# V and U on three shared pairs of PSUM banks, turned modes in the transpose banks, and no filler passes: a sparse-attention and spectral-mixing kernel

## The chip, the cores and the metric

The kernel runs on one core of one Trainium2 chip. The metric is device time in microseconds, the median of several runs. One further execution was recorded by the hardware profiler; it is the source of every time below that is not a median.

The names of the engines in the profile: PE is TensorE (matrix multiplication), PEld its weight loads, DVE is VectorE, ACT is ScalarE, POOL is GpSimd (here it mainly issues the loads that convert float32 to float16), SP issues the stores. PSUM is the small memory that TensorE writes its results to. It has eight banks here, each of 512 float32 values per partition; a "pair" below is two banks that one instruction of ScalarE or VectorE can read in one go.

## The reference

Two stages. First an attention over 8 batches, 8 heads, 576 tokens and 64 dimensions; the first four heads see the last 32 tokens, the last four every 32nd token. Then a spectral mixing of the attention's output `x` (8 x 576 x 512): a Fourier transform along the tokens, of which 64 modes are kept and each multiplied by its own complex 512 x 512 matrix, the inverse transform, and a last layer.

```python
def _attn_ref(q, k, v):
    # B, H, S, D = 8, 8, 576, 64; stride 32
    scores = scale * np.matmul(q, k.transpose(0, 1, 3, 2))
    mask_local = (rel >= 0) & (rel < stride)
    mask_strided = (rel >= 0) & (pos[None, :] % stride == pos[:, None] % stride)
    # ... heads 0 to 3 local, 4 to 7 strided; softmax
    return np.matmul(attn, v)

def _moe_ref(x, w_r, w_i, w_ch):
    X = np.fft.rfft(x, axis=1)
    Xr, Xi = (np.real(X[:, :n_modes]), np.imag(X[:, :n_modes]))   # n_modes = 64
    Yr = np.einsum('bmd,mde->bme', Xr, w_r) - np.einsum('bmd,mde->bme', Xi, w_i)
    Yi = np.einsum('bmd,mde->bme', Xr, w_i) + np.einsum('bmd,mde->bme', Xi, w_r)
    Y[:, :n_modes] = Yr + 1j * Yi
    y = np.fft.irfft(Y, n=S, axis=1)
    u = x + y
    return u + np.maximum(u @ w_ch, 0.0)
```

The weights of the modes, 2 x 64 x 512 x 512 float32 values, are most of what the kernel reads: 162.83 MB come from memory in all.

## The kernel before

In order of time the kernel does this:

1. The strided attention of the eight batches, while the first weights are loaded.
2. The local attention, interleaved with the first modes (`slot` 0), while weights stream in. Each batch ends with a DFT of its output.
3. More modes (`slot` 1), while `premix` prepares for each token tile its share of `x @ w_ch` (called v) and of `x` (xo), with the modes still missing.
4. The last stretch: the last 24 modes. Between them, `renew` adds the modes that are already there to v and xo. The last of the spectra is added in a final loop, which puts out `u + relu(v)` tile by tile. V stands for the accumulation of `u @ w_ch`, U for that of `u`.

PSUM is divided by pools, which change from stage to stage. The last stretch has one V pair, two U pairs and two y banks (2 + 4 + 2); when the modes are done, a second V pair, `v2`, takes the place of y.

```python
    def psum_pools(**bufs):
        pctx.close()
        for n, c in bufs.items():
            pss[n] = pctx.enter_context(
                tc.tile_pool(name="ps_" + n, bufs=c, space=PSUM)
            )
# ...
    psum_pools(y=2, tp=2, sc=2, av=2)      # stages 2 and 3
# ...
    psum_pools(v=1, u=2)                   # stage 4
    yctx = ctx.enter_context(ExitStack())
    pss["y"] = yctx.enter_context(tc.tile_pool(name="ps_y2", bufs=2, space=PSUM))
```

The DFT of a batch, and a pair of modes. Four modes (two pairs) accumulate in one y bank; ScalarE copies it out (`yr`), and `four_turned` turns the result with four small passes through another bank. `flush` calls it at the next odd mode.

```python
    def dft(b, half):
        # ...
        xp = psum("sc" if half else "y")
        # ... ten passes into xp, then four copies by ScalarE from xp to X

    def four_turned(slot, m0, yr):
        tr = psum("y")
        for e in range(4):
            nc.tensor.matmul(
                tr[:, ds(64 * e, 64)].rearrange("p (i x) -> p i x", i=4),
                yr[:, ds(128 * e, 128)],
                idn.rearrange("p (i x h) -> p h i x", i=4, h=2)[:, m0 // 32],
                start=True,
                stop=True,
            )
        # ...

    def mode_pair(slot, m):
        half = 1 - slot
        if m % 4 == 0:
            ypt[slot] = psum("y")
        yp = ypt[slot]
        # ... eight passes wt x X into yp (line 587)
        if slot or m // 2 not in GUEST:
            w_fetch()          # next weights, into the buffer now free
        if m % 4:
            yr = big.tile([128, DM], F16, tag="yr", name="yr")
            act_copy(yr, yp)
            queued.append(lambda: four_turned(slot, m - 2, yr))
```

The last 16 modes take another form: sixteen short passes each (line 620), with the weights as the stationary operand.

The last stretch: the late spectra, the filler and the renewal of one tile pair.

```python
    def spec_late(mm, kept, eng):
        up = psum("u", pair=True)
        for bq in range(2):
            mm(2, bq, up[:, bq])
        for b in range(B):
            eng(kept[b][64:96], up[ds(32 * (b % 4), 32), b // 4])

    def fill(acc, n):
        for _ in range(n):
            nc.tensor.matmul(acc, idn, v0s[0][:, 0], start=True, stop=True)

    def renew(b, ts):
        n = len(ts)
        if n == 2:
            v0, xo = v0s[b][:, ts[0] : ts[0] + 2], xos[b][:, ts[0] : ts[0] + 2]
        else:
            v0, xo = v0h[b // 2].unsqueeze(1), xoh[b // 2].unsqueeze(1)
        vp, up = psum("v", pair=True), psum("u", pair=True)
        if n == 1:
            fill(vp[:, 0], 3)
        for j, t in enumerate(ts):
            nc.tensor.matmul(vp[:, j], idn, v0[:, j], start=True, stop=False)
            rows_of(b, t, vp[:, j], zzs, False)
        act_copy(v0, vp[:, 0:n])
        for j, t in enumerate(ts):
            rows_of(b, t, up[:, j], yys, True)
        nc.vector.tensor_tensor(out=xo, in0=up[:, 0:n], in1=xo, op=AluOp.add)

    def spec_last():
        spec_late(spec_y, yys, lambda o, i: nc.vector.tensor_copy(out=o, in_=i))
        fill(psum("v", pair=True)[:, 0], 5)
```

In `renew`, the identity pass of V has line 949 in the profile, the passes of `rows_of` line 750, `fill` line 937, and the add line 954; `act_copy` has line 243 for all its callers.

The units of the final loop. Their identity passes have lines 985 (V) and 995 (U), those of `new_rows` line 1008. V and U of unit 0, and U of unit 1, are started before the last modes.

```python
    def v_early(k, stop=False):
        vps[k] = psum(("v", "v2")[k % 2], pair=True)
        v_own(k, stop)

    def u_early(k, times=1):
        ups[k] = psum("u", pair=True)
        rows = list(enumerate(own(items[k], xos, xoh)))
        for n, (j, r) in enumerate(rows * times):
            nc.tensor.matmul(
                ups[k][:, j], idn, r, start=True, stop=n < len(rows) * (times - 1)
            )
# ...
    rest = [(0, m) for m in range(SPLIT1, NM)] + [(1, m) for m in range(SPLIT0, NM)]
    n = 0
    NL = len(rest) - 2
    for i, (slot, m) in enumerate(rest):
        mode(slot, m)
        upto = min(len(late), i + 1)
        for w in late[n:upto]:
            w()
        n = upto
        if i == NL - 1:
            v_early(0)
            u_early(0)
        elif i == NL:
            u_early(1, times=3)
    yctx.close()
    # ... the last spectra (spec_z, spec_y), then:
    pss["v2"] = pctx.enter_context(tc.tile_pool(name="ps_v2", bufs=1, space=PSUM))
# ...
    for k in range(2, LAST + 2):
        if k <= LAST:
            v_early(k)
        # ... at k = 4 and 5 half of the V pair serves for the last spectrum
        if k > 2:
            u_early(k - 1)
        if k <= LAST:
            new_rows(k, vps[k], zzs)
        if k > 2:
            new_rows(k - 1, ups[k - 1], yys)
        if k <= LAST:
            v_done(k)          # ScalarE: relu(V)
        # ...
        if k > 2:
            u_done(k - 1)      # VectorE: U + relu(V), then the store
```

Of the kernel before, what the change touches and what calls it, by code (L numbers as in the profile page):

```python
# [56 lines left out]
def kernel(  # L57
# [10 lines left out]
    nc = tc.nc  # L68
# [6 lines left out]
    pss = {}  # L75
    pctx = ctx.enter_context(ExitStack())

    def psum_pools(**bufs):
        pctx.close()
        for n, c in bufs.items():  # L80
            pss[n] = pctx.enter_context(
                tc.tile_pool(name="ps_" + n, bufs=c, space=PSUM)
            )

    def psum(kind, half=False, pair=False):
        if pair:
            return pss[kind].tile([128, 2, 512], FP, tag=kind, name=kind)
        if half:
            return pss[kind].tile([128, 1024], F16, tag=kind, name=kind)
        return pss[kind].tile([128, 512], FP, tag=kind, name=kind)  # L90
# [19 lines left out]
    idn = cs["cI"]  # L110
# [11 lines left out]
    def spectra_tile(n):  # L122
        if n == "X0":
            Xh[0] = big.tile([128, 4, B, 2, NM], F16, tag=n, name=n)
        else:
            YS[n] = big.tile([128, 4, 4, 16, 16], F16, tag=n, name=n)
# [115 lines left out]
    def act_copy(out, in_):  # L242
        nc.scalar.activation(out=out, in_=in_, func=ACTF.Copy)  # L243
# [307 lines left out]
    def spectrum(slot, part, src):  # L551
        if slot == 0:
            nc.scalar.activation(out=YS["Y0"][part], in_=src, func=ACTF.Copy)
        else:
            nc.vector.tensor_tensor(
                out=YS["YT"][part], in0=src, in1=YS["Y0"][part], op=AluOp.add
            )

    def four_turned(slot, m0, yr):
        tr = psum("y")  # L560
        for e in range(4):
            nc.tensor.matmul(
                tr[:, ds(64 * e, 64)].rearrange("p (i x) -> p i x", i=4),
# [5 lines that stand above are left out]
        if slot == 0 and m0 == 0:  # L569
            spectra_tile("Y0")  # L570
        spectrum(
            slot,
            (slice(None), slice(None), m0 // 16, slice(None), ds(m0 % 16, 4)),
            tr[:, 0:256].rearrange("p (e i x) -> p e x i", e=4, i=4),
        )
# [28 lines left out]
    def mode(slot, m):  # L604
        half = 1 - slot
        if m % 2:
            flush()
        if slot == 0 or m < SPLIT0:
            if m % 2:
                mode_pair(slot, m - 1)  # L610
            return
        mi, mg = m % 8, m // 8
        if mi == 0:
            ypt[slot] = psum("y")
        yp = ypt[slot]
        yv = yp.rearrange("p (m e x) -> p m e x", m=8, e=4)
        wt = w_tiles[ORDER.index((half, m))]
        for e in range(4):
            for c in range(4):
                nc.tensor.matmul(  # L620
                    yv[:, mi, e, :],
                    wt[:, XC[c], ds(128 * e, 128)],
                    Xh[half][:, c, :, :, m],
                    start=(c == 0),
                    stop=(c == 3),
                )
        if m % 2:
            w_fetch()
        ends = {5: 6, 7: 2} if mg == 7 else {7: 8}
        if mi in ends:  # L630
            n = ends[mi]
            m0 = mi + 1 - n
            spectrum(
                slot,
                (slice(None), slice(None), mg // 2, slice(None), ds(8 * (mg % 2) + m0, n)),
                yp.rearrange("p (m e x) -> p e x m", m=8, e=4)[:, :, :, ds(m0, n)],
            )
# [54 lines left out]
    v0s, xos = {}, {}  # L692
# [51 lines left out]
    def rows_of(b, t, acc, spectra, fresh):  # L744
        if t < 4:
            todo = [(acc, out_cols(t), b)]
        else:
            todo = [(acc[ds(64 * j, 64)], ds(512, 64), b - 1 + j) for j in range(2)]
        for o, cols, bb in todo:
            nc.tensor.matmul(  # L750
                o, cA[0:96, cols], spectra[bb][0:96], start=fresh, stop=True
            )


    psum_pools(tp=3, sc=3, av=2)
    load_str(0, 1)
    const_load(nc.scalar, "cI", "cM6", "cM5")
# [66 lines left out]


    psum_pools(y=2, tp=2, sc=2, av=2)
    NMODES = [10, 8, 7, 7, 6, 6, 6, 6]
    for b in range(B):
# [12 lines left out]
        n = 0  # L841
        nm = NMODES[b]
        for mi in range(nm):
# [3 lines left out]
            n = upto  # L847
# [7 lines left out]
    xoh = [ptr.tile([128, DM], F16, name=f"xoh{i}") for i in range(4)]  # L855
# [58 lines left out]
    n = 0  # L914
    for m in range(SPLIT0):
# [4 lines left out]
        n = upto  # L920
        if m >= 16 and m % 16 in (2, 4):
            spec(m // 16 - 1, m % 16 // 2 - 1)

    psum_pools(v=1, u=2)
    yctx = ctx.enter_context(ExitStack())
    pss["y"] = yctx.enter_context(tc.tile_pool(name="ps_y2", bufs=2, space=PSUM))

    def spec_late(mm, kept, eng):
        up = psum("u", pair=True)
        for bq in range(2):  # L930
            mm(2, bq, up[:, bq])
        for b in range(B):
            eng(kept[b][64:96], up[ds(32 * (b % 4), 32), b // 4])

    def fill(acc, n):
        for _ in range(n):
            nc.tensor.matmul(acc, idn, v0s[0][:, 0], start=True, stop=True)

    def renew(b, ts):
        n = len(ts)  # L940
        if n == 2:
            v0, xo = v0s[b][:, ts[0] : ts[0] + 2], xos[b][:, ts[0] : ts[0] + 2]
        else:
            v0, xo = v0h[b // 2].unsqueeze(1), xoh[b // 2].unsqueeze(1)
        vp, up = psum("v", pair=True), psum("u", pair=True)
        if n == 1:
            fill(vp[:, 0], 3)
        for j, t in enumerate(ts):
            nc.tensor.matmul(vp[:, j], idn, v0[:, j], start=True, stop=False)
            rows_of(b, t, vp[:, j], zzs, False)  # L950
# [4 lines that stand above are left out]

    def spec_last():
        spec_late(spec_y, yys, lambda o, i: nc.vector.tensor_copy(out=o, in_=i))
        fill(psum("v", pair=True)[:, 0], 5)

    late = [lambda: spec_late(spec_z, zzs, act_copy), spec_last]  # L960
    for b in range(B):
        for t in (0, 2):
            late.append(lambda b=b, t=t: renew(b, (t, t + 1)))
        if b % 2:
            late.append(lambda b=b: renew(b, (4,)))

    def units_of(item):
        P, t = item
        return [(2 * P + j, t) for j in range(2 if t < 4 else 1)]

    items = []
# [5 lines left out]
    vps, ups, rls, osbs = {}, {}, {}, {}  # L977

    def own(item, kept, half):
        P, t = item  # L980
        return [kept[b][:, t] for b, _ in units_of(item)] if t < 4 else [half[P]]

    def v_own(k, stop=False):
        for j, r in enumerate(own(items[k], v0s, v0h)):
            nc.tensor.matmul(vps[k][:, j], idn, r, start=True, stop=stop)  # L985

    def v_early(k, stop=False):
        vps[k] = psum(("v", "v2")[k % 2], pair=True)
        v_own(k, stop)

    def u_early(k, times=1):
        ups[k] = psum("u", pair=True)
        rows = list(enumerate(own(items[k], xos, xoh)))
        for n, (j, r) in enumerate(rows * times):
            nc.tensor.matmul(  # L995
                ups[k][:, j], idn, r, start=True, stop=n < len(rows) * (times - 1)
            )

    def new_rows(k, acc, spectra):
        P, t = items[k]  # L1000
# [46 lines left out]
# [9 lines that stand above are left out]
            v_early(0)  # L1056
            u_early(0)
        elif i == NL:
            u_early(1, times=3)
    yctx.close()  # L1060
    with tc.tile_pool(name="ps_s", bufs=1, space=PSUM) as pss["s"]:
        zp = pss["s"].tile([128, 512], FP, name="zp")
# [16 lines left out]
# [3 lines that stand above are left out]
        if k == 4:  # L1082
            held = vps[k][:, 1]
            spec_z(3, 1, held)
        if k == 5:
            held = vps[k][:, 1]
            spec_y(3, 1, held)
# [7 lines that stand above are left out]
            v_done(k)  # L1095
        if k in (4, 5):
            act_copy((zzs, yys)[k - 4][1], held)
        if k > 2:
            u_done(k - 1)
# [31 lines left out]
```

The softmax here doesn't subtract the row's maximum and nothing guards it: scores larger than these inputs give would overflow.

## Time and profile before

| | |
|---|---|
| median of 3 runs | 432.15 us (431.37 to 432.51) |
| span of the profiled execution | 432.4 us |
| instructions | 9809 |
| mean granted TensorE clock | 0.935 |
| PE busy | 351.0 us (81%), 4188 passes |
| DVE busy | 235.3 us (54%) |
| ACT busy | 218.9 us (51%) |
| POOL busy | 107.8 us (25%) |
| moved by DMA | 91.64 MB, mean 212 GB/s |
| read from and written to memory | 162.83 and 9.44 MB |

How to read it: a busy share is an average over stages that have different limits, so it doesn't tell what a change in one stage is worth. Matmuls are pipelined, and a busy PE is not PE at its peak. The row PEclk of the profile gives the clock that TensorE was granted, in tenths of full speed. A line such as "[1.41 <-ACT X L243]" at the end of a timeline entry says that the engine stood idle for 1.41 us before the instruction, and that the instruction of ScalarE in line 243 which writes or reads X ended the wait. L followed by a number is a line of the kernel; where a helper issues for many callers, all share its line.

### The profile page before, as it was taken

What the parts mean: (1) busy time and instruction counts of PE and PEld (TensorE: products, weight loads), DVE (VectorE), ACT (ScalarE), POOL (GpSimd) and SP (SyncE); (2) the same over time, 40 slices, a digit from 0 to 9 for tenths busy, and PEclk for the clock granted to TensorE, in tenths of its full rate; (3) what the DMA queues carried; (4) which work ended last, traced back from release to release, by engine and by line L of the source; (5) the groups of instructions that cost most, each with busy time, mean ns of one, the idle gap of its engine ahead of it and who ended that gap; (6) DMA issues with size and microseconds to landing.
All of it is one profiled execution on the core that took longest, in us unless ns stands there. A gap on an engine that the chain in (4) does not pass through costs nothing.

```text
span 432.4 us, 9809 instructions
## 1 busy us (share of the span) xinstructions
PE 351.0 (81%) x4188; PEld 208.2 (48%) x4188; DVE 235.3 (54%) x467; ACT 218.9 (51%) x393; POOL 107.8 (25%) x191
## 2 busy tenths in 40 slices
PE   2977878779889998887676689886988788798993
PEld 2765767635455656554333344443444334444331
DVE  3888768834253545443213347735864554443784
ACT  1776768633565575656433325422633653342772
POOL 7333332321322332222222222222222222110000
PEclk9999989967898999999988889989999998879997
DMA  8999999999999999999999999999999999991697
GB/s 150 212 212 212 213 214 210 212 211 212 183 210 215 213 213 212 215 215 213 212 213 214 213 215 214 213 213 213 213 215 213 214 214 212 214 210 30 241 362 273
DMA packets 30475, 91.64 MB, mean 212 GB/s; under 512 B 4000, under 2 KB 4768, under 8 KB 30432
## 3 DMA queue, kind: packets, MB, share of 16 engines
q0 software_dynamic: 24704, 81.28, 95.1%
q1 hardware_dynamic: 5216, 9.52, 6.2%
q8 instruction: 33, 0.54, 0.5%
q10 hardware_dynamic: 512, 0.21, 0.2%
q14 instruction: 10, 0.08, 0.0%
HBM read 162.83 MB, written 9.44 MB: 398 GB/s over the span
## 4 chain that ended last, share of the span: by engine, by line
DMA 57%; PE 29%; DVE 5%; ACT 5%; issue 3%; POOL 0%; DVEq 0%; ACTq 0%; POOLq 0%
DMA wt<-in_moe_w_i_dram 39%; DMA ring<-in_q_dram 7%; PE y L587 6%; DMA w_ch<-in_moe_w_ch_dram 5%; DMA wt<-in_moe_w_r_dram 4%; PE tp L405 3%; ACT X L243 2%; PE v L985 2%; PE u L995 2%; PE sc L451 2%; DMA ring<-in_k_dram 2%; DVE xb L233 2%; PE y L524 1%; PE sc L467 1%; PE v L1008 1%
## 5 line engine op out<-in xcount | busy, mean ns | idle before, releaser
L587 PE MATMUL y<-wt,X 128*32 128x512 f16 (+1 forms) x448 | 72.2, 428 | 24.4 <-DMA wt<-in_moe_w_i_dram 18.5
L178 POOL DMA_DIRECT2D wt<-in_moe_w_r_dram x62 | 36.5, 589 | 157.2 <-PE y L587 78.7
L587 PEld LDWEIGHTS <-X 128*32 128x32 f16 (+1 forms) x448 | 29.1, 139 | 45.1 <-issue 20.1
L178 POOL DMA_DIRECT2D wt<-in_moe_w_i_dram x60 | 35.6, 594 | 59.6 <-DMA wt<-in_moe_w_i_dram 53.5
L717 DVE COPY xo<-tp 128x512 f16<-128x512 f16 x32 | 22.1, 690 | 37.2 <-PE tp L715 37.1
L716 ACT ACTIVATE v<-sc 128x512 f16<-128x512 f32 x32 | 19.1, 597 | 45.8 <-PE sc L707 45.7
L481 ACT ACTIVATE PL<-sc 128x480 f16<-128x480 f32 (+1 forms) x48 | 26.6, 578 | 26.6 <-PE sc L467 26.4
L707 PE MATMUL sc<-w_cp,xT 128*128 128x512 f16 x128 | 36.5, 407 | 1.9 <-DVE xT L680 1.9
L233 DVE TENSOR_TENSOR xb<-av,rec 90x256 f16<-90x256 f32 (+2 forms) x80 | 36.0, 450 | 2.8
L412 DVE COPY qT<-tp 128x576 f16<-128x576 f16 x16 | 12.0, 757 | 42.0 <-PE tp L405 39.0
L243 ACT ACTIVATE yr<-y 128x512 f16<-128x512 f32 x28 | 16.7, 597 | 31.8 <-PE y L587 31.6
L954 DVE TENSOR_TENSOR xo<-u,xo 128x1024 f16<-128x1024 f32 x16 | 19.5, 1224 | 19.1 <-PE u L750 19.1
L232 DVE RECIPROCAL rec<-av 90x4 f32<-90x4 f32 (+2 forms) x80 | 14.6, 182 | 27.9 <-PE av L496 18.4
L370 ACT ACTIVATE PL<-sc 90x360 f16<-90x360 f32 (+1 forms) x48 | 22.7, 489 | 7.7 <-PE sc L363 7.3
L243 ACT ACTIVATE v<-v 128x1024 f16<-128x1024 f32 x16 | 16.4, 1025 | 20.2 <-PE v L750 20.2
L1030 DVE TENSOR_TENSOR osb<-u,rl 128x1024 f32<-128x1024 f32 (+1 forms) x21 | 22.2, 1071 | 5.5 <-PE u L1008 3.4
L243 ACT ACTIVATE v<-tp 128x640 f16<-128x640 f16 (+1 forms) x24 | 18.8, 806 | 11.4 <-PE tp L439 8.7
L405 PE MATMUL tp<-cI_s,ring 64*64 64x64 f16 x864 | 23.3, 199 | 0.8 <-DVE qT L412 0.6
L268 PE MATMUL tp<-cI_s,ring 72*128 72x72 f16 x256 | 15.4, 207 | 8.7 <-DMA ring<-in_v_dram 7.3
L405 PEld LDWEIGHTS <-ring 64*64 64x64 f16 x864 | 18.2, 113 | 8.4 <-issue 4.6
L1022 ACT ACTIVATE rl<-v 128x1024 f32<-128x1024 f32 (+1 forms) x21 | 18.8, 902 | 6.6 <-PE u L1008 4.1
L451 PE MATMUL sc<-cMl_s,cI_s 128*128 128x480 f16 (+1 forms) x48 | 19.4, 403 | 2.5 <-ACT X L243 1.6
(139 smaller groups left out, 732.7 us busy)
## 6 DMA issues: line engine op xcount, KB each, us to landing
wt<-in_moe_w_r_dram POOLq DMA_DIRECT2D x62, 512.0 KB, 18.5
wt<-in_moe_w_i_dram POOLq DMA_DIRECT2D x60, 512.0 KB, 19.0
out_dram<-osb SPq DMA_DIRECT2D x15, 512.0 KB, 3.2
ring<-in_v_dram POOLq DMA_DIRECT2D x8, 288.0 KB, 12.7
ring<-in_q_dram POOLq DMA_DIRECT2D x8, 288.0 KB, 12.8
ring<-in_k_dram POOLq DMA_DIRECT2D x8, 288.0 KB, 12.3
ring<-in_v_dram POOLq DMA_DIRECT2D x3, 512.0 KB, 15.0
ring<-in_q_dram POOLq DMA_DIRECT2D x3, 512.0 KB, 14.7
```

The lines of the kernel that those rows point to most:

```text
L178: nc.gpsimd.dma_start(dst, rows)
L233: nc.vector.tensor_tensor(out=dst, in0=val.rearrange("p h (q c) -> p h c q", c=4), in1=rec[0:n, 0:pieces] .to_broadcast((n, pieces, 64)) . ...
L243: nc.scalar.activation(out=out, in_=in_, func=ACTF.Copy)
L370: nc.scalar.activation(out=PS[0:n, ds(POFF[t], 4 * n)], in_=scp[0:n, 0 : 4 * n], func=ACTF.Exp, scale=SCALE,)
L405: nc.tensor.transpose(tp[ds(64 * hp, 64), ds(64 * i, 64)], qn[ds(64 * hp, 64), ds(64 * (9 * g + i), 64)], idn[ds(64 * hp, 64), ds(64 * hp, ...
L451: nc.tensor.matmul(scp[:, 0 : n * times].rearrange("p (h x) -> p h x", h=times), idn, mask_rows("cMl", n, times), start=True, stop=False,)
L481: nc.scalar.activation(out=dst, in_=src, func=ACTF.Exp, scale=SCALE)
L587: nc.tensor.matmul(yp[ds(a, 32), :], Xh[half][pr, c].rearrange("p b r (h m) -> p (b r h) m", h=2)[:, :, mm % 32], wt[pr, XC[c], :], start= ...
L707: nc.tensor.matmul(vp, xT[:, ch], w_chs["cp"][:, ch, :], start=(ch == 0), stop=(ch == 3),)
L717: nc.vector.tensor_copy(out=xo.rearrange("p (h q c) -> p h q c", h=2, c=4), in_=tp[:, 0:512].rearrange("p (h c q) -> p h q c", h=2, c=4),)
L954: nc.vector.tensor_tensor(out=xo, in0=up[:, 0:n], in1=xo, op=AluOp.add)
L1030: nc.vector.tensor_tensor(out=osb[:, j], in0=up[:, j], in1=rl[:, j], op=AluOp.add)
```

## The change

It has three parts.

- The last stretch has one pool `p` of three pairs in place of one V pair and two U pairs. V and U take the next pair of the rotation in the order in which they are asked for. The idea is that V no longer has to wait for its only pair to be read out.
- While the attention's transpose banks `tp` exist (stages 2 and 3), `four_turned` takes one of them rather than a y bank, so that the two y banks alternate between the modes themselves and the DFTs. `pss.clear()` makes the test `"tp" in pss` true only while the pool is there.
- The passes that only fill time are gone: `fill`, which put 3 or 5 identity passes into a V bank whose result is overwritten, and the repeated start of U of unit 1 (`times=3`).

```diff
--- before.py
+++ after.py
@@ -77,6 +77,7 @@
 
     def psum_pools(**bufs):
         pctx.close()
+        pss.clear()
         for n, c in bufs.items():
             pss[n] = pctx.enter_context(
                 tc.tile_pool(name="ps_" + n, bufs=c, space=PSUM)
@@ -557,7 +558,7 @@
             )
 
     def four_turned(slot, m0, yr):
-        tr = psum("y")
+        tr = psum("tp" if "tp" in pss else "y")
         for e in range(4):
             nc.tensor.matmul(
                 tr[:, ds(64 * e, 64)].rearrange("p (i x) -> p i x", i=4),
@@ -921,20 +922,16 @@
         if m >= 16 and m % 16 in (2, 4):
             spec(m // 16 - 1, m % 16 // 2 - 1)
 
-    psum_pools(v=1, u=2)
+    psum_pools(p=3)
     yctx = ctx.enter_context(ExitStack())
     pss["y"] = yctx.enter_context(tc.tile_pool(name="ps_y2", bufs=2, space=PSUM))
 
     def spec_late(mm, kept, eng):
-        up = psum("u", pair=True)
+        up = psum("p", pair=True)
         for bq in range(2):
             mm(2, bq, up[:, bq])
         for b in range(B):
             eng(kept[b][64:96], up[ds(32 * (b % 4), 32), b // 4])
-
-    def fill(acc, n):
-        for _ in range(n):
-            nc.tensor.matmul(acc, idn, v0s[0][:, 0], start=True, stop=True)
 
     def renew(b, ts):
         n = len(ts)
@@ -942,9 +939,7 @@
             v0, xo = v0s[b][:, ts[0] : ts[0] + 2], xos[b][:, ts[0] : ts[0] + 2]
         else:
             v0, xo = v0h[b // 2].unsqueeze(1), xoh[b // 2].unsqueeze(1)
-        vp, up = psum("v", pair=True), psum("u", pair=True)
-        if n == 1:
-            fill(vp[:, 0], 3)
+        vp, up = psum("p", pair=True), psum("p", pair=True)
         for j, t in enumerate(ts):
             nc.tensor.matmul(vp[:, j], idn, v0[:, j], start=True, stop=False)
             rows_of(b, t, vp[:, j], zzs, False)
@@ -955,7 +950,6 @@
 
     def spec_last():
         spec_late(spec_y, yys, lambda o, i: nc.vector.tensor_copy(out=o, in_=i))
-        fill(psum("v", pair=True)[:, 0], 5)
 
     late = [lambda: spec_late(spec_z, zzs, act_copy), spec_last]
     for b in range(B):
@@ -985,16 +979,13 @@
             nc.tensor.matmul(vps[k][:, j], idn, r, start=True, stop=stop)
 
     def v_early(k, stop=False):
-        vps[k] = psum(("v", "v2")[k % 2], pair=True)
+        vps[k] = psum(("p", "v2")[k % 2], pair=True)
         v_own(k, stop)
 
-    def u_early(k, times=1):
-        ups[k] = psum("u", pair=True)
-        rows = list(enumerate(own(items[k], xos, xoh)))
-        for n, (j, r) in enumerate(rows * times):
-            nc.tensor.matmul(
-                ups[k][:, j], idn, r, start=True, stop=n < len(rows) * (times - 1)
-            )
+    def u_early(k):
+        ups[k] = psum("p", pair=True)
+        for j, r in enumerate(own(items[k], xos, xoh)):
+            nc.tensor.matmul(ups[k][:, j], idn, r, start=True, stop=False)
 
     def new_rows(k, acc, spectra):
         P, t = items[k]
@@ -1056,7 +1047,7 @@
             v_early(0)
             u_early(0)
         elif i == NL:
-            u_early(1, times=3)
+            u_early(1)
     yctx.close()
     with tc.tile_pool(name="ps_s", bufs=1, space=PSUM) as pss["s"]:
         zp = pss["s"].tile([128, 512], FP, name="zp")
```

## The prediction

> **What bounds the kernel now.** I read the page's forty slices first, then the chain that ended last, then the timeline of the stretches where the slices change.
>
> The slices (10.8 us each), rows for TensorE, its granted clock, the DMA engines and their rate:
>
> ```profile
> PE   2977878779889998887676689886988788798993
> ...
> PEclk9999989967898999999988889989999998879997
> DMA  8999999999999999999999999999999999991697
> GB/s 150 212 212 212 213 214 210 212 211 212 183 210 215 213 213 212 215 215 213 212 213 214 213 215 214 213 213 213 213 215 213 214 214 212 214 210 30 241 362 273
> ```
>
> From slice 1 to slice 35 (11 to 389 us) the rate stands at 210 to 215 GB/s whatever TensorE does. The loads of attention inputs and weights bound these 380 us, with one hole: slice 10 (108 to 119 us) has 183. After 389 us the loads fade, and what follows is TensorE and stores. The chain says the same:
>
> ```profile
> DMA 57%; PE 29%; DVE 5%; ACT 5%; issue 3%; POOL 0%; DVEq 0%; ACTq 0%; POOLq 0%
> ```
>
> In order of time this chain runs weight load after weight load from 175 to 373.8 us, and from 373.92 to the end it is TensorE with its evacuations. So only two places can give time: the hole at 110 to 118 us, because it delays every later load, and everything after 373.92 us.
>
> The second place, from the timeline (start, duration, engine, line, idle before and what ended it):
>
> ```profile
> 379.57 1.45 PE L937 MATMUL v<-v,cI_s 128*128 128x512 f16 x3
> ...
> 385.05 0.38 PE L949 MATMUL v<-v,cI_s 128*128 128x512 f16 x1 [0.20 <-ACT v L243]
> ...
> 386.12 1.02 ACT L243 ACTIVATE v<-v 128x1024 f16<-128x1024 f32 x1 [1.12 <-PE v L750]
> ...
> 387.19 0.38 PE L949 MATMUL v<-v,cI_s 128*128 128x512 f16 x1 [0.20 <-ACT v L243]
> ...
> 391.48 0.81 PE L937 MATMUL v<-v,cI_s 128*128 128x512 f16 x3 [0.20 <-ACT v L243]
> ...
> 394.39 0.64 PE L620 MATMUL y<-X,wt 128*128 128x16 f16 x16
> 394.87 1.46 PE L995 MATMUL u<-xo,cI_s 128*128 128x512 f16 x6
> ...
> 396.16 0.59 PE L620 MATMUL y<-X,wt 128*128 128x16 f16 x16
> ```
>
> One renewal plus one mode repeats every 387.19 - 385.05 = 2.14 us: with a single V pair the next V group can't start before ScalarE has emptied the last (1.02 us). L937 and four of the six L995 are passes that only fill time. The last two modes run at 394.39 and 396.16. When were their weights there? The last load was issued at 383.53:
>
> ```profile
> 383.53 0.52 POOL L182 DMA_DIRECT2D wt<-in_moe_w_i_dram  x1 [1.92 <-DMA wt<-in_moe_w_i_dram]
> ```
> ```profile
> wt<-in_moe_w_i_dram POOLq DMA_DIRECT2D x1, 256.0 KB, 9.6
> ```
>
> It landed at 383.53 + 9.6 = 393.1. The one before that matters, issued at 378.70 with 12.0 us to landing, was there at 390.7. TensorE is 3.7 and 3.0 us late on the last two modes.
>
> The first place, in the first local-attention batch:
>
> ```profile
> 112.07 1.55 ACT L243 ACTIVATE X<-y 64x256 f16<-64x256 f32 x4 [1.14 <-PE y L524]
> ...
> 113.67 1.92 PE L587 MATMUL y<-wt,X 128*32 128x512 f16 x8 [1.41 <-ACT X L243]
> ...
> 115.89 0.59 POOL L178 DMA_DIRECT2D wt<-in_moe_w_r_dram  x1 [4.89 <-PE y L587]
> ```
>
> The modes of L587 stood 1.41 us because their y bank was the one that the DFT had filled, and ScalarE had to empty it. Their end freed the weight buffer that the next load was waiting for. The load rate over 100 to 125 us in 40 parts of 0.625 us shows what that costs:
>
> ```profile
> GB/s 221 203 221 199 218 220 214 199 201 236 220 210 213 211 223 210 184 184 111 190 197 197 210 223 203 210 138 125 118 177 210 203 216 216 210 216 187 191 203 214
> ```
>
> **What the Trainium skill says.** "TensorE: Matmul & The Clock Gate", Part 1: TensorE's clock is full or half, decided over free-running windows of 3413 ns, and an idle window halves it. Part of that agrees: the clock row of the stretches has 0.50 for 376.2 to 383.0 (two such windows), and 512-column passes start 0.42 us apart there against 0.215 at full clock. Its section "Why this matters for your kernels" gives about 3 us of idle as the safe gap; the trace is stricter. The half-clock spells at 359.1 and 376.2 follow gaps of only 1.43 and 1.81 us. "PSUM — Partial Sum Buffer", Specifications: eight banks of 2 KiB. Three pairs and two y banks fill them, so the change can't give V and U more than six; it only deals them differently. Nothing in a page says what a bank rotation is worth.
>
> **The change part by part.**
>
> *Turned modes in the transpose banks.* Before, the y banks of the first batch go in turn to modes, turned modes, modes, DFT, turned modes, modes: the last collides with the DFT. Without the turned modes the order is modes, modes, DFT, modes, and the last takes the bank read out at 109.6 to 110.2 us. The 1.41 us wait goes, and the eight passes can start at 112.2. They took 1.92 us at half clock (113.3 to 116.7 us is a half-clock spell) and 1.08 at full; with less idle the spell may not come. The weight buffer is free at about 113.4 instead of 115.8, so the loads are issued some 2.4 us earlier, and the trough of 138, 125, 118, 177 goes. Against 213 it misses (75+88+95+36) x 0.625 us = 184 KB, or 0.86 us of loading. I count 0.8, and it moves every later load. The other DFTs have no hole behind them; with eight loads of 18 to 20 us in flight they only change slack. Turned modes cost a transpose bank for one 0.38 us copy every four modes; the local stage waits for loads, so I count nothing.
>
> *Rotation and fillers before the last mode.* From 376 us on TensorE is late, so what it sheds is on the path until it meets the loads.
> - Waits for the V pair: 0.20 at 376.55, 385.05, 387.19, 389.34 and 391.48, and 0.47 at 393.53: 1.5 us.
> - Filler passes: three at half clock (3 x 0.427 = 1.28), three at full (3 x 0.215 = 0.65), four of U (0.86): 2.8 us.
>
> Sum 4.3 us. The earlier eleven passes (five in the late spectra, three each at 352.75 and 366.27) lie ahead of waits for weights and give nothing. Rebuilt from the mode at 384.21: it is ready at about 383.4 (weights landed 383.3), a step is six passes of 0.215 plus 0.64 = 1.93 us, so the next modes come at 385.4, 387.3 and 389.3; then the short renewal (0.65) and V and U of unit 0 (0.86) put the second to last at 391.4 and its U pass done at 392.5. There the last weights (393.1) bind: the last mode runs at 393.3 instead of 396.16. Of 4.3 us shed, 2.9 arrive at the end and 1.3 turn into waiting.
>
> *Rotation in the last loop.* Units there take 1.30 us, six passes of 0.215, V on alternating pairs and U on two. With three shared pairs and the separate second V pair the sequence settles to the same: U3 waits for V2 instead of U1, V4 for U1 instead of V2, later each for its own predecessor. I count 0.
>
> Sum: 0.8 + 2.9 = 3.7 us, all ahead of a last loop that merely shifts: 428.4 us.
>
> **Rivals.**
> - *A cold last loop.* The fillers may have bought the full clock. The trace has both signs:
>
> ```profile
> 372.70:376.20 3.50, 2.29 (x38) 1.60 (x39) 0.96 (x2) 0.76 (x2) 0.52 (x1) 0.99 1.07 215
> 376.20:383.00 6.80, 6.61 (x53) 2.64 (x50) 3.26 (x4) 1.92 (x3) 1.55 (x3) 0.50 1.07 213
> ...
> 396.60:400.00 3.40, 2.50 (x20) 1.04 (x16) 1.02 (x3) 1.26 (x3) 0.00 (x0) 1.00 0.00 0
> ```
>
>   A window with 2.29 us busy of 3.5 was followed by half clock; one with 2.50 of 3.4, full of short gaps, was not. After the change the last mode stands for 0.8 us and the gaps of the spectrum copies follow. One half-clock window in a loop bound by TensorE costs half of 3.41, 1.7 us; two cost 3.4 and leave nearly nothing (about 432). I give one such window an even chance: +0.8 on the mean, 429.2 us.
> - *The loads don't move.* Eight outstanding loads may hide the hole's issues; against it stands that the rate really fell. Then 430.0.
> - *A new wait in the rotation.* The second renewal's V now follows VectorE's yy copies (until 346.7, its V started at 345.91). That costs 0.8 us ahead of a later wait of 1.43 us for weights, so it should vanish. If adds on VectorE (1.22 us) held V back at every renewal, the gain of 2.9 would shrink to about 2 and the time be near 430.
> - *The stores bind.* They run at 342 GB/s in the last loop and end 4.5 us after the last issue; started earlier they end earlier. No change.
>
> **Range and chances.** 428.4 with a warm loop, about 430 with one cold window, 429.2 between. Low: the hole closes fully and a half-clock spell at 376 also goes (1.5 us more): 427.0. High: two cold windows, or no earlier loads with one: 431.8. Two per cent are 8.6 us, more than both places together hold, and nothing in the change adds that much work either: 0.02 for each side.
>
> **What would show it.** Right: no wait for ScalarE's X ahead of L587 near 112 us and no rate under 180 near 117; the last weights landing near 392.3; no 0.20 us waits for V in the renewals; the last mode near 392.5 right after its weights; the first store issue near 397 instead of 400.69. Wrong: half clock between 393 and 405 us, the last loop longer than its 26 us, V or U groups waiting for VectorE, or the last weights no earlier than 393.

## The result

| | before | after |
|---|---|---|
| median, first comparison | 431.64 us (430.81 to 432.51, 6 runs) | 429.78 us (429.08 to 430.12, 6 runs) |
| ratio, 95% interval | | 0.9953 (0.9937 to 0.9969) |
| the same comparison later | 431.79 us (56 runs) | 430.21 us (22 runs), ratio 0.9966 (0.9953 to 0.9980) |
| span of the profiled execution | 432.4 us | 428.0 us |
| last weights land | 393.2 us | 392.4 us |
| last mode starts | 396.16 us | 392.56 us |
| first store issued | 400.69 us | 397.13 us |

The change takes 0.3 to 0.5% off, 1.5 to 2 us. The two profiles differ by 4.4 us, more than twice that. Which of the two numbers is the change is the first question of this case. A span is about 1.8 us shorter than the time of the same execution: the profiled one of before took 434.14 us, 2.5 more than the median, and that of after took 429.78 us, just the median. So 2.5 of the 4.4 us belong to that one execution of the kernel before, not to the change.

In the kernel after, the lines stand a little further down: the modes are L588 and L621, the renewals L944 and L751, V and U of the last loop L979, L988 and L999. Its slices, and the first line of its chain:

```profile
PE   2976888779999997997666789877879888878994
...
PEclk9999899967999998999888889999989988899999
DMA  8999999999999999999999999999999999994698
GB/s 149 209 212 213 213 213 212 211 211 212 207 211 215 212 214 214 214 214 214 211 214 214 214 212 214 214 212 214 214 213 214 213 213 214 214 212 84 227 356 300
```
```profile
DMA 61%; PE 24%; DVE 6%; ACT 4%; issue 3%; DVEq 0%; POOL 0%; ACTq 0%; POOLq 0%
```

Slice 10 went from 183 to 207 GB/s. In the chain TensorE gave up five points and DMA gained four: followed in time, it now runs along weight loads as far as 392.56 us, but for 4 us of TensorE at 358 and 2.4 us around the issue of the last load at 380, where before it had left them at 373.92. The end of the stretch, by the timeline:

```profile
386.21 0.64 PE L621 MATMUL y<-X,wt 128*128 128x16 f16 x16
...
387.99 0.64 PE L621 MATMUL y<-X,wt 128*128 128x16 f16 x16
...
390.33 0.64 PE L621 MATMUL y<-X,wt 128*128 128x16 f16 x16
390.81 0.59 PE L988 MATMUL p<-xo,cI_s 128*128 128x512 f16 x2
392.56 0.64 PE L621 MATMUL y<-X,wt 128*128 128x16 f16 x16 [1.16 <-DMA wt<-in_moe_w_i_dram]
```

The last mode waits 1.16 us for its weights. No V group waits any more for ScalarE to empty its pair, and a renewal with its mode repeats every 1.78 us (386.21 to 387.99), where the prediction had worked out 1.93: a mode holds TensorE for 0.48 us (390.33 to 390.81), not for the 0.64 that its line shows. The first batch of the local attention:

```profile
111.62 1.55 ACT L244 ACTIVATE X<-y 64x256 f16<-64x256 f32 x4 [1.14 <-PE y L525]
111.74 1.08 PE L588 MATMUL y<-wt,X 128*32 128x512 f16 x8
...
113.12 0.58 POOL L179 DMA_DIRECT2D wt<-in_moe_w_r_dram  x1 [2.57 <-PE y L588]
```
```profile
GB/s 214 206 206 220 210 225 188 221 205 217 227 205 217 208 223 216 190 184 177 190 210 203 229 203 223 210 210 223 210 216 210 210 210 227 188 204 211 206 214 207
```

The modes start beside ScalarE's copies of X, not after them, and the trough of 118 to 138 GB/s near 117 us is gone from the rate over 100 to 125 us. An earlier one, at 110 to 112 us, is still there (190, 184 and 177; before it was 184, 184 and 111).

### The profile page after: what moved, and what is told of

Its sections match the earlier page's. It is cut to its first block, busy times and chain, and to the rows that moved or that the text cites. A ratio compares the mean times of both kernels' runs of the same rounds, so it can differ in the third digit from the quotient of the medians.

```text
span 428.0 us, 9765 instructions
## 1 busy us (share of the span) xinstructions
PE 345.7 (81%) x4167; PEld 205.5 (48%) x4167; DVE 235.1 (55%) x467; ACT 218.4 (51%) x393; POOL 107.5 (25%) x191
## 4 chain that ended last, share of the span: by engine, by line
DMA 61%; PE 24%; DVE 6%; ACT 4%; issue 3%; DVEq 0%; POOL 0%; ACTq 0%; POOLq 0%
DMA wt<-in_moe_w_i_dram 46%; DMA wt<-in_moe_w_r_dram 9%; PE y L588 5%; DMA ring<-in_q_dram 4%; PE tp L406 2%; DVE xb L234 2%; DMA ring<-in_k_dram 2%; PE sc L452 2%; PE p L988 2%; PE p L999 1%; PE sc L468 1%; DVE kz L276 1%; PE y L525 1%; PE v L979 1%; DMA ring<-in_v_dram 1%
## 5 line engine op out<-in xcount | busy, mean ns | idle before, releaser
L588 PE MATMUL y<-wt,X 128*32 128x512 f16 (+1 forms) x448 | 72.6, 431 | 21.0 <-DMA wt<-in_moe_w_i_dram 20.8
L588 PEld LDWEIGHTS <-X 128*32 128x32 f16 (+1 forms) x448 | 28.3, 140 | 42.7 <-DMA wt<-in_moe_w_i_dram 21.1
L949 DVE TENSOR_TENSOR xo<-p,xo 128x1024 f16<-128x1024 f32 x16 | 19.6, 1225 | 19.3 <-PE p L751 19.1
L244 ACT ACTIVATE v<-p 128x1024 f16<-128x1024 f32 x16 | 16.4, 1023 | 19.6 <-PE p L751 19.5
L1021 DVE TENSOR_TENSOR osb<-p,rl 128x1024 f32<-128x1024 f32 (+1 forms) x21 | 22.2, 1071 | 5.5 <-PE p L999 3.4
L244 ACT ACTIVATE kz<-tp 64x360 f16<-64x360 f16 (+1 forms) x32 | 18.9, 591 | 1.9 <-PE tp L406 1.0
```

Of the source, the lines that this page charges most:

```text
L588: nc.tensor.matmul(yp[ds(a, 32), :], Xh[half][pr, c].rearrange("p b r (h m) -> p (b r h) m", h=2)[:, :, mm % 32], wt[pr, XC[c], :], start= ...
L1021: nc.vector.tensor_tensor(out=osb[:, j], in0=up[:, j], in1=rl[:, j], op=AluOp.add)
```

## The experiments

My theory had two parts: the loads come 0.8 us earlier because the turned modes left the y banks, and TensorE is no longer late at the last mode because V's wait and the fillers went. Against it stood: the loads carry nearly all of the gain; the lag hides the loads; the fillers had bought the full clock. Each ratio is to the kernel before on the same chip, with its 95% interval. A difference of 0.001 between two of them says nothing: for three kernels measured side by side (the change with all fillers kept, with fillers in the last gap, and twice the fillers) the plain medians, over 431.91 us, give 0.9974, 0.9968 and 1.0030 in place of 0.9958, 0.9954 and 1.0023. Twelve kernels ran, and their profiles are set side by side further down. "Late" is the time by which the last mode starts after its weights have landed; a "spell" is an unbroken time at half clock, made of windows of 3.41 us.

**Only the turned modes moved.**

```diff
-        tr = psum("y")
+        tr = psum("tp" if "tp" in pss else "y")
```

> Only the turned modes move to the transpose banks; fillers and the one V pair stay. Two-part theory (earlier loads and a TensorE lag ahead of the last modes are separate gains): the last weights land 0.8 us earlier, near 392.4, and the end moves by the same 0.8 us; ratio 0.998; the last mode still starts 2 to 3 us after its weights. Rival (the loads carry nearly all of the measured 1.9 us): ratio 0.9955 to 0.9965. Rival (the lag hides it): ratio 1.000, last weights earlier, end unchanged.

Measured: 1.0003 (0.9993 to 1.0012), not the 0.998 of the theory. Its last weights landed at 392.0 and the last mode started at 394.35. The end didn't move at all: the rival in which the lag hides the loads holds here. Its waits of TensorE from 373 us on show why:

```profile
PE y L621 <- DMA wt<-in_moe_w_i_dram: 1.3, 1, 1.3
PE v L950 <- ACT v L244: 0.8, 4, 0.2
```

It waited once more for weights, and then again for its single V pair.

**Only the rotation.**

```diff
-    psum_pools(v=1, u=2)
+    psum_pools(p=3)
-        vp, up = psum("v", pair=True), psum("u", pair=True)
+        vp, up = psum("p", pair=True), psum("p", pair=True)
```

(and the same in the spectra, the fillers, V and U of the last loop)

> Only the rotation of three shared pairs; all fillers stay, turned modes stay in y. Two-part theory: the five waits of 0.2 us for the V pair and the 0.47 us wait of V of unit 0 go, 1.5 us at most, so ratio 0.9965 to 0.998; last weights unchanged near 393. Rival (V and U get in each other's way on shared pairs): waits of V for VectorE appear and the ratio is 1.000 or above.

Measured: 0.9967 (0.9954 to 0.9980), 1.4 us; last mode 0.5 us after its weights. The waits for the V pair are gone, and no wait of V for VectorE has come. A renewal with its mode takes 1.78 us here too, fillers or not:

```profile
384.99 0.64 PE L620 MATMUL y<-X,wt 128*128 128x16 f16 x16
...
386.77 0.64 PE L620 MATMUL y<-X,wt 128*128 128x16 f16 x16
```

This one part does most of what the whole change does.

**Only the fillers removed.**

```diff
-        if n == 1:
-            fill(vp[:, 0], 3)
-        fill(psum("v", pair=True)[:, 0], 5)
-            u_early(1, times=3)
+            u_early(1)
```

> Only the 21 filler passes go; one V pair, turned modes in y. Two-part theory: up to 2.8 us of passes leave the path, capped by the last weights; ratio 0.994 to 0.997. Rival (the fillers bought the full clock): half-clock spells appear between 383 and 405 us that the kernel before doesn't have, and the ratio is 1.000 to 1.004.

Measured: 0.9993 (0.9980 to 1.0006), not told apart from nothing, and not the 0.994 to 0.997 of the theory. One of the 14 runs, a slow one of 437.75 us, is left out. The profile has half clock at 346.2 to 353.0, 370.1 to 376.9 and 383.7 to 387.1, 17.1 us against 10.2 in the kernel before. One of the three lies where the rival put it. The runs agree: the mean granted clock is 0.930 in the other 13, and 0.942 in 27 runs of the kernel before beside them.

**Rotation and no fillers, turned modes in y.** The two diffs above together.

> Rotation and no fillers, turned modes still in y. Two-part theory: the last mode starts as its weights land, near 393.2, so 2 to 3 us less than before at the end less a possible cold window; ratio 0.9955 to 0.9975, and this plus the part of the turned modes gives the whole change (0.9953). Rival (the loads carry nearly all): ratio 0.999 to 1.000.

Measured: 0.9957 (0.9942 to 0.9973), inside what the two-part theory expected; the last mode started 0.1 us after its weights. Without any help from the turned modes this is all of the 0.9953 (a repetition further down gave 0.9971).

**The kernel before again.** No edit.

> The kernel before, unchanged, for its spread and a second profile. Theory: ratio 1.000; its profiled span of 432.4 us was at the slow end of its own spread because two half-clock windows fell at 376 to 383 us, so in a second profile the last mode stands less late, 1 to 3 us, and the span is nearer 430. Rival: the span is 432 again and the gap between profile and median lies elsewhere.

Measured: 1.0001 (0.9990 to 1.0012), profiled span 429.9 us. Its clock was half at 359.5 to 369.8 and full from there on:

```profile
382.41 0.64 PE L620 MATMUL y<-X,wt 128*128 128x16 f16 x16 [0.46 <-DMA wt<-in_moe_w_i_dram]
...
385.03 0.38 PE L949 MATMUL v<-v,cI_s 128*128 128x512 f16 x1 [0.20 <-ACT v L243]
...
391.37 0.59 PE L985 MATMUL v<-v,cI_s 128*128 128x512 f16 x2 [0.47 <-ACT v0h L243]
```

So TensorE could still wait for weights at 382.41, and was late only after that: its last mode started at 394.00, 1.7 us after the last weights (392.3). In the first profile, with two half-clock windows at 376.2 to 383.0, it was 3.0 us after weights that landed 0.9 us later (393.2). The profile of before was an unlucky execution of it, and the 4.4 us between the first two profiles are not the change.

**The whole change with all fillers kept.** The diffs of the turned modes and of the rotation.

> The whole change but with all 21 filler passes kept. Theory that lag counts: the fillers on the path cost what the loads don't hide, so 0.5 to 1.5 us more than the whole change; ratio 0.9965 to 0.9985 to the kernel before. Rival (fillers keep the clock full): as fast as or faster than the whole change, ratio 0.994 to 0.9955.

Measured: 0.9958 (0.9939 to 0.9976). Between the two expectations (by the medians, inside the first), and not told apart from the whole change.

**Fillers only in the last gap.** The whole change, with

```diff
-            u_early(1)
+            u_early(1, times=3)
```

> The whole change, with only the four filler passes of U of unit 1 put back, 0.86 us in the gap of 1.16 us in which TensorE waits for the last weights. Theory: they fit in the gap and cost nothing, and a warmer last loop is worth nothing measurable; ratio 0.9953 within 0.001. Rival (a cold window at the start of the last loop costs 1.7 us in half of the executions): 0.8 us faster, ratio near 0.9935.

Measured: 0.9954 (0.9935 to 0.9973), as expected; the rival's 0.9935 lies at the very edge of the interval. No gain from a last loop warmed in this way was seen.

**Twice the fillers.** The kernel before, with

```diff
-            fill(vp[:, 0], 3)
+            fill(vp[:, 0], 6)
-        fill(psum("v", pair=True)[:, 0], 5)
+        fill(psum("v", pair=True)[:, 0], 10)
-            u_early(1, times=3)
+            u_early(1, times=5)
```

> The kernel before with the fillers doubled: 6 in place of 3 in each short renewal, 10 in place of 5 after the late spectra, 8 in place of 4 extra passes of U of unit 1. Theory that TensorE is late before the last modes: the added passes behind 376 us, 6 x 0.215 to 0.43 and 4 x 0.215, lie on the path: 2.1 to 2.8 us longer, ratio 1.005 to 1.0065. Rival (fillers ride in waits for weights, or buy clock): ratio 1.000 to 1.002.

Measured: 1.0023 (1.0013 to 1.0032), 1.0 us longer (1.3 by the medians): between the two. The passes are on the path (the last mode was 3.3 us late), but the profile has no half clock at all between 300 and 425 us, where the kernel before had 10 us of it. That would fit fillers which cost what they take and give back part of it as clock; the run doesn't separate the two.

**The whole change again.** No edit to the kernel after.

> The whole change again, for its spread and beside the next kernel on the same chip. Theory: ratio 0.9953 within 0.001, the last mode within 1 us of its weights.

Measured: 0.9966 (0.9953 to 0.9980), span of the profile 429.8 us. The expected window (0.9943 to 0.9963) was missed by the estimate, and the last mode was 1.6 us late. Three stretches of its profile (duration; busy time and number of instructions of PE, PEld, DVE, ACT and POOL; then clock, DMA share, GB/s), the mode at the end of the second, and the modes of the third:

```profile
373.00:376.40 3.40, 3.40 (x45) 1.92 (x42) 2.76 (x3) 1.44 (x3) 1.03 (x2) 1.00 1.06 213
376.40:379.80 3.40, 1.37 (x22) 0.72 (x21) 1.48 (x2) 0.84 (x1) 0.52 (x1) 1.00 1.07 214
379.80:390.10 10.30, 10.30 (x88) 4.77 (x85) 3.87 (x4) 3.67 (x4) 1.03 (x2) 0.50 1.01 201
```
```profile
378.64 0.64 PE L621 MATMUL y<-X,wt 128*128 128x16 f16 x16 [2.03 <-DMA wt<-in_moe_w_i_dram]
...
383.06 0.68 PE L621 MATMUL y<-X,wt 128*128 128x16 f16 x16
...
386.09 0.68 PE L621 MATMUL y<-X,wt 128*128 128x16 f16 x16
...
389.12 0.68 PE L621 MATMUL y<-X,wt 128*128 128x16 f16 x16
```

With no fillers and no waits for V, TensorE catches up with the loads early, waits 2.03 us for weights (1.37 us busy of 3.40), and then runs three windows at half clock. There a step takes 3.03 us (386.09 to 389.12), while weights for a mode come every 2.46 us (0.5 MB at 213 GB/s). It fell behind again.

**The same with the turned modes in y, beside it.** The edit is that of rotation and no fillers.

> The whole change with the turned modes back in y, beside the whole change. Theory that the 0.6 us by which the loads come earlier reaches the end once TensorE is not late: 0.5 to 0.7 us slower than the whole change, ratio to the kernel before 0.0012 to 0.0016 higher. Rival (it gets lost again, as with the turned modes alone): equal within 0.0005.

Measured: 0.9971 (0.9954 to 0.9988), 0.0005 above the whole change, less than the expected 0.0012 to 0.0016; the intervals are too wide to say that it is nothing. What the turned modes give at the end is 0 to 0.5 us. The two slices rows are more telling than the times. First this kernel, then the whole change again:

```profile
PEclk9999999969989999998958899999999989697998
...
GB/s 156 209 212 214 212 214 212 211 211 211 214 212 215 213 213 214 214 213 213 213 213 213 213 215 213 214 213 213 214 213 213 214 213 214 213 213 61 226 354 302
```
```profile
PEclk9999999956999999999986889999989989868998
...
GB/s 152 212 213 213 213 212 212 211 211 211 186 207 214 213 214 214 213 214 214 212 213 214 214 214 214 214 213 214 214 213 213 214 213 214 214 212 71 227 353 300
```

The kernel with the turned modes in y has no hole in slice 10 (214), and the one that moved them has it (186). But it is not the hole that the prediction named. The rate of the whole change again over 100 to 125 us:

```profile
GB/s 210 214 206 218 199 214 220 214 211 217 217 220 211 210 210 216 177 125 79 131 170 190 216 197 236 190 216 203 170 203 197 203 190 203 203 227 188 202 202 210
```

Its trough lies at 110 to 113 us; near 117 us a single 170 is left.

**Turned modes and no fillers, one V pair.**

> Turned modes in the transpose banks and no fillers, but one V pair. Theory that V's single pair sets the pace of the renewals: the gain stays small, ratio 0.997 to 1.000, the mean granted clock stays near 0.93, and the waits of V for ScalarE are all there. Rival (fillers were what kept TensorE late): ratio 0.9955 or below.

Measured: 0.9964 (0.9948 to 0.9980). Better than either of its parts alone, and outside the expected window by its estimate though not by its interval; mean granted clock 0.937 where I expected about 0.93. The profile has its last mode 1.3 us late, as without the turned modes (1.4), but its last weights at 392.0 in place of 392.9. Why the earlier loads reach the end here and not with the fillers isn't settled.

**Fillers where TensorE waits for weights.** The whole change, with four passes into the next renewal's V pair ahead of modes 8, 10, 12, 14, 16 and 18 of the last 24:

```diff
+        if i in (7, 9, 11, 13, 15, 17):
+            nextvp.append(psum("p", pair=True))
+            fill(nextvp[0][:, 0], 4)
```

> The whole change with four filler passes ahead of each of six modes that stand first in a weight pair (modes 8 to 18 of the last 24), where TensorE waits 1.1 to 1.9 us for weights. Theory that fillers buy clock and cost only where TensorE is late: mean granted clock up by 0.005 to 0.010 against the whole change, and 0 to 0.5 us faster than it. Rival (0.86 us of passes push the modes): 0.3 to 1 us slower than the whole change.

Measured: 1.0007 (0.9988 to 1.0026), some 1.8 us behind the whole change on the same chip (0.0041 of 432). The clock rose as expected, from 0.930 to 0.940 on the mean; the time missed both expectations. The 22 runs spread from 429.68 to 434.64 us. Up to the last mode the fillers did what they were for: full clock from 349.6 to 394.0, last mode at 392.01, the earliest of all. Then the cold loop came, here:

```profile
390.00:394.00 4.00, 2.41 (x38) 1.35 (x35) 0.29 (x1) 0.00 (x0) 0.00 (x0) 1.00 0.11 23
394.00:400.80 6.80, 6.46 (x23) 1.41 (x21) 3.21 (x4) 3.73 (x5) 0.00 (x0) 0.50 0.23 86
400.80:424.00 23.20, 23.16 (x137) 7.32 (x136) 18.50 (x17) 16.68 (x19) 0.00 (x0) 1.00 0.88 314
```

From the last mode to the last pass of TensorE it took 31.55 us. In the other thirteen profiles that is 29.00 to 29.11 (to the start of that pass). Two windows at half clock cost 2.5 us. The whole change in its first profile had the same kind of gap just before, without that end. First the window before the cold loop, then two of the whole change:

```profile
390.60:394.00 3.40, 1.81 (x23) 1.05 (x23) 0.29 (x1) 0.00 (x0) 0.00 (x0) 1.00 0.06 12
```
```profile
388.90:392.30 3.40, 2.43 (x26) 1.10 (x24) 1.58 (x3) 0.60 (x1) 0.00 (x0) 1.00 0.35 69
392.30:395.70 3.40, 2.24 (x28) 1.42 (x28) 0.98 (x2) 0.60 (x1) 0.00 (x0) 1.00 0.00 0
```

**All profiles side by side.** Times in us from the start. "Half clock" is the time at half clock between 340 us, where the first fillers stand, and 424 us; "spell" is the last unbroken one that ends before 105 us. The last two columns are the load rates, in GB/s, of 108 to 114 us and of 114 to 121 us.

| kernel | ratio | last weights | last mode | late by | half clock | spell | 108 to 114 | 114 to 121 |
|---|---|---|---|---|---|---|---|---|
| before | | 393.2 | 396.16 | 3.0 | 10.2 | 89.4 to 103.1 | 193 | 183 |
| before again | 1.0001 | 392.3 | 394.00 | 1.7 | 10.2 | 89.9 to 103.5 | 196 | 192 |
| twice the fillers | 1.0023 | 392.2 | 395.46 | 3.3 | 0 | 85.4 to 95.7 | 214 | 211 |
| turned modes | 1.0003 | 392.0 | 394.35 | 2.3 | 3.4 | 90.9 to 94.3 | 213 | 212 |
| rotation | 0.9967 | 392.8 | 393.28 | 0.5 | 6.8 | 89.5 to 103.1 | 201 | 191 |
| turned modes and rotation | 0.9958 | 392.4 | 392.83 | 0.5 | 6.8 | 91.2 to 94.6 | 215 | 212 |
| no fillers | 0.9993 | 392.9 | 394.29 | 1.4 | 17.1 | 90.2 to 103.8 | 196 | 191 |
| turned modes, no fillers | 0.9964 | 392.0 | 393.30 | 1.3 | 13.7 | 90.0 to 93.4 | 215 | 212 |
| rotation, no fillers | 0.9957 | 393.2 | 393.34 | 0.1 | 13.7 | 90.2 to 103.9 | 190 | 181 |
| the same again | 0.9971 | 391.7 | 393.17 | 1.5 | 17.1 | 83.6 to 93.8 | 214 | 213 |
| whole change | 0.9953 | 392.4 | 392.56 | 0.1 | 10.2 | 88.5 to 102.2 | 201 | 214 |
| whole change again | 0.9966 | 392.8 | 394.39 | 1.6 | 17.1 | 86.3 to 103.4 | 169 | 202 |
| fillers in the last gap | 0.9954 | 391.9 | 392.81 | 0.9 | 17.1 | 92.2 to 95.6 | 209 | 213 |
| fillers in the waits | 1.0007 | 391.9 | 392.01 | 0.1 | 10.2 | 90.2 to 93.6 | 213 | 212 |

The span of an execution is close to a sum: last weights, plus lag, plus 29 us of loop, plus 6.2 to 7.2 us until the end.

## Why the prediction was right, and where not

The time was predicted as 429.2 us in a range of 427.0 to 431.8; it is 429.78, and 430.21 in the repetition. The path was right: the loads bind up to the last weights, TensorE's lag comes on top, and then a loop that only shifts. That the number came so near is in part luck: the gain was put at 2.9 us and is 1.5 to 1.9, and 0.8 us set aside for a cold loop, which the change didn't show, covered part of a lag read too large. Step by step:

- **The X wait ahead of the modes.** Right as far as the instructions go. It stands in all seven profiles with turned modes in y (1.4 us each) and in none of the seven without. The issue of the next weights came at 113.12 in place of 115.89.
- **0.8 us of loading.** Half of this step failed. I took the wait as the cause of the hole, and it is not enough by itself: in both profiles with turned modes in y and a spell that ended at 95.7 or 93.8 us the wait is there and no hole follows (211 to 214 GB/s). It takes a late start too. In all seven profiles with a spell to 102 us or later the second mode pair starts 7.29 us after the first, in the other seven 4.55 to 4.65. The late ones have a hole at 108 to 114 us wherever the turned modes go (169 to 201 GB/s), which I hadn't counted; the five of them with turned modes in y also have the one near 117 us that I had (181 to 192), and the two that moved them don't (214 and 202). Moving the turned modes can't have made or shortened a spell: in all fourteen profiles the first turned mode starts only after the spell has ended (at 104.99 us against 103.1 in the kernel before). So the term is about right in an execution with a long spell and nothing in one without. At the end of the kernel the move gave nothing alone (1.0003) and 0.0004 to 0.0009 next to the rotation, which the intervals don't tell from zero.
- **1.5 us of waits for V.** Right in the sum: the rotation alone took 1.4 us. The parts were read too small, since a step fell from 2.14 to 1.78 us, by 0.36 and not by the 0.20 of idle time that the timeline shows.
- **2.8 us of fillers.** Counted right as passes, wrong as time. Taken out alone they gave 0.0007 (0.3 us), next to the rotation 0.0010 (0.9967 to 0.9957), next to both other parts nothing clear (0.9958 to 0.9953 or 0.9966). Only next to the turned modes did they give 0.0039 (1.0003 to 0.9964). I had put the clock risk into the last loop only; it came in the renewals. The six profiles with all or more fillers have 0 to 10.2 us of half clock after 340 us, the eight without, or with some in other places, 10.2 to 17.1. At half clock a step of 3.03 us can't follow loads of 2.46.
- **2.9 us at the end.** The cap by the last weights was right as a rule: 0.1 to 0.5 us of lag with the rotation in five profiles of eight. But 2.9 was the lag of one execution, which took 434.14 us, and I subtracted it from a median of 432.15. The second profile of the same kernel has 1.7, which is about the change's gain. The term was mis-sized because one profile was read as the kernel.
- **The last loop counts 0.** Right: 29.06 us before, 29.05 after.
- **Rivals.** The cold last loop is real and costs 2.5 us for two windows (predicted 3.4), but it showed in one of fourteen profiles, and not in those of the change itself; an even chance was too much. V waiting for VectorE's copies at 346 us didn't come: the second renewal did start at 346.98 against 345.91, but without a wait, behind a mode at half clock (1.92 us against 1.08). One wait of V for VectorE's adds shows, 0.65 us at 348.10 with rotation and no fillers. The loads not moving is near the truth in the times. The stores never bound.

What stays open: why the turned modes without fillers did better (0.9964) than either alone, so that there the gain comes without the rotation, and how much of the 0.3 to 0.5% is theirs. Cold loops in other executions of the kernel with fillers in the waits would fit its wide spread, but only one execution was profiled.

## What to carry to other kernels

A lag behind a stream of loads can be removed only once, and further savings become waiting: here the rotation alone took 1.4 us, turned modes and no fillers 1.6 us, and all three together 1.5 to 2. Measure such parts together before adding them. Before a gain is read from one profile, take a second one of the same kernel, above all where the clock changed near the end. And a hole in the load rate is to be read together with the clock in the 20 us ahead of it before the nearest wait is blamed.

## What the runs showed of the hardware

Removing the passes that only fill time lengthened TensorE's half-clock time: mean granted clock 0.930 in 13 runs without them against 0.942 in 27 of the kernel before, and 0.930 in 22 runs of the whole change against 0.942 in 56. Waits of 1.4 to 2 us for weights are enough: half clock followed waits of 1.43 and 1.81 us in the kernel before and of 2.03 us in the whole change. The Trainium skill ("TensorE: Matmul & The Clock Gate", section "Why this matters for your kernels") puts the gap to avoid at about 3 us; the measurement is stricter.

The busy time of a window tells most of it. Cut into windows of 3.41 us in step with the half-clock spells, the fourteen profiles have 278 windows at full clock that begin between 338 and 417 us. The 31 that were followed by half clock had 0.92 to 2.34 us of TensorE busy; the 234 with more than that were all followed by full clock. Between 1.78 and 2.34 us both occurred (18 and 13), so busy time alone doesn't settle it.

Doubling the fillers kept the clock full from 300 us to the end of the last loop in the profiled execution, and the kernel still lost 1.0 us: a full clock is not a gain by itself.
